# Attention with head mixing: when loaded operands are split, how early they are fetched, and which steps carry a tile's scores

## The chip, the cores and the metric

The kernel runs on one core of a Trainium2 chip. TensorE multiplies matrices into PSUM; VectorE (DVE), ScalarE (ACT) and GpSimd (POOL) work elementwise; SyncE (SP) issues most of the DMAs, in order, from one queue. The metric is the device time of one execution in microseconds (us); lower is better.

## The reference

```
scores = einsum("bhij,hg->bgij", (q @ k^T) / 8, w_pre)     # batch 4, 12 heads, 448 tokens, head size 64
attn   = softmax(scores)                                    # over j
attn   = einsum("bhij,hg->bgij", attn, w_post)
x      = (attn @ v) as [1792, 768]
h      = x @ w_in                                           # then a first feed-forward block, 2048 wide
y      = (h - tanh(h)) @ w_out
out    = y routed to the best of 8 experts by cosine, relu(y @ w1) @ w2, times the expert's probability
```

All is 32-bit floating point. The change lies in the attention alone.

## The kernel before, in words

The program is unrolled Python. A scheduler lays out each engine's instructions: it goes by the order in which they are written, but may place one ahead of others on its engine when it takes its inputs to be ready, and it inserts the waits. On the chip each engine then works strictly through its own list.

Attention handles one batch after the other. A batch has four tiles of query rows (120, 120, 120 and 88), and a tile is worked in *steps* of 10 rows with all 12 heads: 12, 12, 12 and 9 steps, 45 in a batch, 180 in all. Step numbers here count through the program.

- **Scores** (`scores`, L203 to L209). For a pair of heads, six matmuls make q·k from halves kept in 16 bits (qh, ql, kh, kl). The two results go to PSUM banks 0 and 1, are copied into the tile's `S` by ACT (L209), or by DVE (L207) for heads 2, 5, 8 and 11, and only then can the next pair use the banks. Six pairs make a tile; they are spread over the steps of the tile before it.
- **Gather** (`shuffle`, L231). A DMA on the SP queue collects the 120 rows (10 rows by 12 heads) of one step from `S` into `G`. There are four `G` buffers, so the gather of step s + 4 waits until step s has read its own.
- **Premix** (`premix`, L240 to L255). One matmul with `w_pre` into one of three banks, a minimum over j on DVE (L244), the exponential on ACT (L250, followed by a read of its sum), and on odd steps a subtraction on POOL (L255) that makes a second 16-bit half.
- **Normalise and postmix** (L265 to L295). Four steps later, `w_post` scaled by the sums multiplies the transposed exponentials: 4 fp32 matmuls on even steps (the trace counts 8 passes), 12 on 16-bit halves on odd ones. ACT copies the result into `at32` (L294), POOL makes its low half (L295). The banks are 4 and 5 in turn.
- **Values** (`window`, `values`, L305 to L313). When a batch's 45 steps are through, 144 matmuls multiply by v.

Into these steps work is placed that loads and *splits* operands. A fetch issues a DMA on the SP queue into one of three `raw` buffers; a split casts it on ACT and subtracts on POOL or DVE, and so frees the buffer: `fetch_v`/`split_v` (L192, L193), `fetch_pairs`/`split_pairs` for the next batch's q and k (L171 to L177), `fetch_w`/`convert_w` for w_in of the later feed-forward block (three DVE operations L77 to L81, an ACT cast L326, a DVE subtraction L327, and two DMAs out, L350). The table `todo` holds which of them run in which step: `at(s, f, ...)`. A split follows its fetch by 4 steps for v, 2 for q and k, 3 for w_in. Before a step's own work, the loop issues gathers for steps up to s + 3, but those of a new tile only from two steps before its first.

Of the kernel before, what the change touches and what calls it, by code (L numbers as in the profile page):

```python
# [16 lines left out]
AF = mybir.ActivationFunctionType  # L17
ALU = mybir.AluOpType
AX = mybir.AxisListType
# [3 lines left out]
B, H, S, D = 4, 12, 448, 64  # L23
# [11 lines left out]
GB = 4  # L35
# [4 lines left out]
AHEAD = 4  # L40
# [16 lines left out]
def group(t, c):  # L57
    i0, m, _ = TILES[t]
    if m == 120:
        return [i0 + c + 12 * ii for ii in range(10)]  # L60
    if c < 8:
        return [i0 + c + 8 * ii for ii in range(10)]
    return [i0 + 80 + ii for ii in range(8)]
# [26 lines left out]
def halved(u):  # L90

    return u % 2 == 1


def attention(tc, bank, q0, k0, qT, kT, vP, w_pre, w_post, w_in, xd, wind, pos, yg, constants):
    nc = tc.nc
    HW = DM // 2
    with ExitStack() as ctx:
# [121 lines left out]
        def shuffle(b, t, c):  # L220
            i0, m, _ = TILES[t]
            g = gp.tile([120, S], F32, tag="G", name=f"G_{b}_{t}_{c}")
            s = St[b, t]
            n = len(group(t, c))
            if m == 120:
                rows = s[c:c + 12 * 9 + 1:12]
            elif c < 8:
                rows = s[c:c + 8 * 9 + 1:8]
            else:
                rows = s[80:88]  # L230
            nc.sync.dma_start(out=g[:12 * n], in_=rows)  # L231
            G[b, t, c] = g

        mid, sums = {}, {}

        def premix(b, t, c, u):
            r = 12 * len(group(t, c))
            g = G.pop((b, t, c))
            ps = bank((2, 3, 6)[u % 3], 0, 1)
            nc.tensor.matmul(ps[:r, :S], wmix[:r, :r], g[:r], start=True, stop=True)  # L240
            if u % 2 == 0:
                sums[u // 2] = p4.tile([120, 8], F32, tag="st", name=f"st_{u // 2}")
            st, k = sums[u // 2], u % 2
            nc.vector.tensor_reduce(out=st[:r, k:k + 1], in_=ps[:r, :S], axis=AX.X, op=ALU.min)  # L244
            bias = st[:r, k:k + 1]
            if halved(u):
                bias = st[:r, 2 + k:3 + k]
                nc.vector.tensor_scalar(out=bias, in0=st[:r, k:k + 1], scalar1=EXPB, scalar2=None, op0=ALU.add)
            a = A[u % (LAG + 1)]
            nc.scalar.activation(out=a[:r, :S], in_=ps[:r, :S], func=AF.Exp, bias=bias, scale=-1.0,  # L250
                                 accum_out=st[:r, 4 + k:5 + k])
            parts = None
            if halved(u):
                parts = a.bitcast(BF)[:, 1::2], a.bitcast(F16)[:, 0::2]
                nc.gpsimd.tensor_tensor(out=parts[1][:r, :S], in0=a[:r, :S], in1=parts[0][:r, :S], op=ALU.subtract)  # L255
            mid[u] = (a, parts)
# [73 lines left out]
        steps = [(b, t, c) for b in range(B) for t in range(4) for c in range(TILES[t][2])]  # L330
        tiles = [(b, t) for b in range(B) for t in range(4)]
        todo = {}

        def at(s, f, *a):
            todo.setdefault(s, []).append((f, a))

        at(30, load_constants)
        for b in range(B):
            s0 = 45 * b
            for jc in range(4):  # L340
                at(s0 + 1 + 4 * jc, fetch_v, b, jc)
                at(s0 + 5 + 4 * jc, split_v, b, jc)
            if b + 1 < B:
                for u in range(NP // 2):
                    at(s0 + 23 + 4 * u, fetch_pairs, b + 1, u)
                    at(s0 + 25 + 4 * u, split_pairs, b + 1, u)

        def store(pairs):
            for o, i in pairs:
# [20 lines left out]
        in_window, u = {}, 0  # L370
        for b in range(B):
            for k in range(4 if b < B - 1 else 5):
                at(45 * b + 10 + 7 * k, fetch_w, u)
                at(45 * b + 13 + 7 * k, convert_w, u)
                u += 1
            n = 5 if b < B - 1 else 0
            in_window[b] = list(range(u, u + n))
            u += n
        assert u == 2 * FC

        first = {}
        s0 = 0
        for ti, (b, t) in enumerate(tiles):
            first[b, t] = s0
            if ti + 1 < len(tiles):
                ng = TILES[t][2]
                for p in range(NP) if ti else range(AHEAD // 2, NP):
                    at(s0 - 3 + (2 * p + 1) * ng // H if ti else 2 * p - AHEAD, scores, *tiles[ti + 1], p)
            s0 += TILES[t][2]

        def after(s):
            if s % 2 == 0 and 0 <= s - 2 < len(steps):
                normalise([u for u in (s - 2, s - 1) if u < len(steps)])
            if s >= LAG:
                postmix(*steps[s - LAG], s - LAG)
                if steps[s - LAG][1:] == (3, 8) and steps[s - LAG][0] < B - 1:
                    window(steps[s - LAG][0])
# [12 lines left out]
            scores(0, 1, p)  # L410
        nxt = 0
        for s, (b, t, c) in enumerate(steps):
            while nxt < min(s + GB, len(steps)) and first[steps[nxt][:2]] <= s + 2:
                shuffle(*steps[nxt])
                nxt += 1
            premix(b, t, c, s)
            for f, a in todo.pop(s, []):
                f(*a)
            after(s)
        assert not todo  # L420
# [643 lines left out]
def talking_heads_moe(ctx, tc, q0, k0, q, k, v, w_pre, w_post, w_in, w_out, emb, tau, w12, ident_d, tri_d, tokf_d, rowi_d,  # L1064
# [11 lines left out]
    def bank(base, i=None, n=2):  # L1076

        if i is None:
# [11 lines left out]
    ids0 = gc.tile([EARLY[1], EARLY[0]], I32, tag="ids0", name="ids0")  # L1090
    chosen = {}
    attention(tc, bank, q0, k0, q, k, v, w_pre, w_post, w_in, xd, wind, pos, yg,
              ((ident, ident_d), (tokf, tokf_d), (rowi, rowi_d), (iota, iota_d), (thr, thr_d)))
    before = moe1(tc, ctx, bank, xd, wind, w_out, emb, tau, (ident, tri_d, tokf, rowi, iota, thr), yg, pos, keep, ids0,
# [59 lines left out]
```

## Time and profile before

| | |
|---|---|
| median of three runs | 1286.94 us |
| lowest, highest | 1285.57, 1294.75 us |
| the profiled execution | 1288.26 us, of which its span is 1286.0 us |
| stepped part of attention in it | 20.1 to 455.8 us |

The rows read from the profile below are of that one execution. Its time lies 1.3 us over the median. "Waits" rows give an engine's idle time by what ended it; a name such as "PE bank L203" is the engine, the tile that is written and the line of the program.

### The profile page before, as it was taken

Reading aid. Unit: us, or ns where it says so; the run is one execution under the profiler, and the core shown is the slowest. Engines: PE = TensorE matmul, PEld = TensorE weight load, DVE = VectorE, ACT = ScalarE, POOL = GpSimd, SP = SyncE. Lnnn points to the kernel's source line nnn. Section 1 sums busy time; section 2 is a strip of 40 time slices with the busy share of each in tenths; the row PEclk is TensorE's granted clock in tenths of the full one; section 3 lists DMA queues with packets and bytes.
Section 4 is the critical chain, followed back from the end, with each engine's and each line's share of the span. In section 5 each row is a group of like instructions: output and inputs, shape, how many; then the busy total and the mean of one; then the engine's idle time right before and its main releaser. Section 6 shows DMA issues by size and latency. Waiting matters only on the chain.

```text
span 1286.0 us, 23742 instructions
## 1 busy us (share of the span) xinstructions
PE 1193.8 (93%) x8624; PEld 837.4 (65%) x8648; DVE 855.1 (66%) x1895; ACT 729.0 (57%) x1499; POOL 707.3 (55%) x594
## 2 busy tenths in 40 slices
PE   8999899989999988999899999999978899999995
PEld 3655565555555664566566666667876678989883
DVE  5877687768767829977766456745878345566662
ACT  6777687667767744444455444545556334555551
POOL 5887678577767753433443335334566355566550
PEclk8999999999999999999999999999998999999998
DMA  6555746555574476223001000100043656678640
GB/s 212 174 182 146 221 162 190 175 182 184 148 208 162 116 236 219 93 97 131 25 1 50 1 25 1 50 1 1 2 140 133 212 194 205 213 242 263 229 159 22
DMA packets 82854, 173.90 MB, mean 135 GB/s; under 512 B 12155, under 2 KB 60155, under 8 KB 82728
## 3 DMA queue, kind: packets, MB, share of 16 engines
q1 hardware_dynamic: 76986, 160.75, 38.7%
q0 software_dynamic: 5472, 11.43, 3.0%
q8 instruction: 70, 1.15, 0.4%
q14 instruction: 56, 0.46, 0.1%
q10 hardware_dynamic: 270, 0.12, 0.0%
HBM read 110.79 MB, written 23.30 MB: 104 GB/s over the span
## 4 chain that ended last, share of the span: by engine, by line
PE 59%; DVE 16%; DMA 12%; ACT 6%; issue 3%; POOL 2%; SPq 0%; POOLq 0%; ACTq 0%; DVEq 0%
PE bank L561 11%; PE bank L533 10%; PE bank L913 7%; PE bank L240 7%; PE bank L937 7%; PE bank L290 7%; DMA G<-S 3%; PE bank L203 3%; DMA raw_v<-in_v_dram 3%; PE bank L305 2%; DVE g L547 2%; DMA wor<-in_w_out_dram 2%; DVE g L548 2%; DVE wl_a L903 2%; ACT A L250 1%
## 5 line engine op out<-in xcount | busy, mean ns | idle before, releaser
L561 PE MATMUL bank<-ghl,whl 128*128 128x512 f32 (+1 forms) x1152 | 258.1, 376 | 9.3 <-POOL ghl L551 4.9
L561 PEld LDWEIGHTS bank<-ghl,whl 128*128 128x128 f32 x1152 | 199.6, 192 | 50.8 <-POOL ghl L551 6.3
L483 POOL TENSOR_TENSOR whl<-wo,whl 128x768 fp32r<-128x768 f32 x64 | 118.8, 1857 | 177.2 <-ACT whl L482 177.1
L295 POOL TENSOR_TENSOR at<-at 128x480 f16<-128x480 f32 x180 | 177.0, 996 | 51.9 <-ACT at L294 50.2
L240 PE MATMUL bank<-G,wmix 120*120 120x448 f32 x360 | 176.7, 575 | 11.3 <-DMA G<-S 11.3
L290 PE MATMUL bank<-wr,A 120*128 120x120 f32 (+4 forms) x1800 | 175.3, 246 | 5.2 <-ACT x L312 3.0
L250 ACT ACTIVATE A<-bank,st 120x448 f32<-120x448 f32 x180 | 114.3, 636 | 53.5 <-DVE st L244 22.2
L244 DVE TENSOR_REDUCE st<-bank 120x1 f32<-120x448 f32 x180 | 111.2, 618 | 46.3 <-PE bank L240 45.1
L903 POOL TENSOR_TENSOR wl_a<-wr_a,wh_a 128x768 bf16<-128x768 f32 x56 | 93.1, 1670 | 70.4 <-ACT wh_a L902 70.0
L551 POOL TENSOR_TENSOR ghl<-g,ghl 128x512 fp32r<-128x512 f32 (+1 forms) x64 | 76.6, 1197 | 99.7 <-ACT ghl L550 99.7
L903 DVE TENSOR_TENSOR wl_a<-wr_a,wh_a 128x768 bf16<-128x768 f32 x56 | 83.1, 1484 | 61.9 <-ACT wh_a L902 61.9
L533 PEld LDWEIGHTS <-wih 128*128 128x128 f16 x768 | 72.4, 99 | 76.3 <-issue 15.9
L290 PEld LDWEIGHTS bank<-wr,A 120*128 120x128 f32 (+1 forms) x720 | 94.5, 198 | 34.5 <-issue 17.8
L294 ACT COPY at<-bank 128x480 f32<-128x480 f32 x180 | 101.3, 567 | 25.0 <-PE bank L290 24.7
L902 ACT CAST wh_a<-wr_a 128x768 f16<-128x768 f32 x112 | 92.6, 829 | 39.2 <-PE bank L937 35.2
L543 DVE SCALAR_TENSOR_TENSOR g<-bank,u 128x512 f32<-128x512 f32 (+1 forms) x64 | 39.9, 623 | 108.6 <-ACT d L540 105.2
L255 POOL TENSOR_TENSOR A<-A 120x448 f16<-120x448 f32 (+1 forms) x90 | 84.4, 938 | 32.0 <-ACT A L250 13.4
L482 ACT CAST whl<-wo 128x768 fp32r<-128x768 f32 x64 | 53.1, 831 | 71.1 <-PE bank L561 53.0
L533 PE MATMUL bank<-mxh,wih 128*128 128x512 f16 (+1 forms) x384 | 85.1, 358 | 5.4 <-DVE d L544 4.2
L290 PEld LDWEIGHTS <-A 120*128 120x128 bf16 (+2 forms) x1080 | 63.1, 100 | 40.9 <-issue 33.9
L550 ACT CAST ghl<-g 128x512 fp32r<-128x512 f32 (+1 forms) x64 | 36.2, 566 | 91.6 <-DVE g L548 81.0
L913 PE MATMUL bank<-xph_a,wh_a 128*128 128x208 f16 (+5 forms) x336 | 87.2, 262 | 0.0
(214 smaller groups left out, 2701.3 us busy)
## 6 DMA issues: line engine op xcount, KB each, us to landing
wr_a<-in_w_dram SPq DMA_DIRECT2D x64, 768.0 KB
G<-S SPq DMA_DIRECT2D x176, 210.0 KB
raw_w<-in_w_in_dram SPq DMA_DIRECT2D x32, 384.0 KB
wor<-in_w_out_dram SPq DMA_DIRECT2D x16, 768.0 KB
raw_v<-in_v_dram SPq DMA_DIRECT2D x16, 384.0 KB
yg<-row SPq DMA_DIRECT2D x3, 1540.0 KB
raw_q<-in_q_dram SPq DMA_DIRECT2D x9, 448.0 KB
raw_k<-in_k_dram SPq DMA_DIRECT2D x9, 448.0 KB
```

The lines of the kernel that those rows point to most:

```text
L240: nc.tensor.matmul(ps[:r, :S], wmix[:r, :r], g[:r], start=True, stop=True)
L244: nc.vector.tensor_reduce(out=st[:r, k:k + 1], in_=ps[:r, :S], axis=AX.X, op=ALU.min)
L250: nc.scalar.activation(out=a[:r, :S], in_=ps[:r, :S], func=AF.Exp, bias=bias, scale=-1.0, accum_out=st[:r, 4 + k:5 + k])
L290: nc.tensor.matmul(ps[:, jc * r:jc * r + r], x[:r, js], w[:r].rearrange("p (a b) -> p a b", b=10)[:, :, :n], start=(i == 0), stop=(i == le ...
L294: nc.scalar.copy(at32[:, :, t0:t0 + n], v)
L295: nc.gpsimd.tensor_tensor(out=atl[:, :, t0:t0 + n], in0=at32[:, :, t0:t0 + n], in1=ath[:, :, t0:t0 + n], op=ALU.subtract)
L483: nc.gpsimd.tensor_tensor(out=w[:, 1], in0=wo[f], in1=w[:, 0].bitcast(F32), op=ALU.subtract)
L533: nc.tensor.matmul(h, u[f][:, c], X[b][v][:, c, :N], start=(i == 0), stop=(i == len(seq) - 1))
L561: nc.tensor.matmul(Y[b][c][:, :N], w[:, u, 128 * c:128 * c + 128], hl[:, v, :N], start=(f == 0 and i == 0), stop=(f == FC - 1 and i == 2))
L902: nc.scalar.copy(wh, raw)
L903: (nc.vector if j else nc.gpsimd).tensor_tensor(out=wl, in0=raw, in1=wh, op=ALU.subtract)
L913: nc.tensor.matmul(h, w[u][:, 128 * c:128 * c + 128], XP[e][v][:, c, :N], start=(i == 0), stop=(i == len(seq) - 1))
```

## The change

Four things. The splits are wrapped in `behind`, which ties every instruction that a split puts on DVE or ACT behind the step's own minimum (DVE) and exponential (ACT); in a step's list they now run ahead of the other entries. The splits and fetches move: v is fetched in steps 5, 9, 13, 17 of a batch (it was 1, 5, 9, 13) and split 4 steps later as before; q and k are fetched in the same steps 23, 27, 31 but split 4 steps later, not 2; w_in is fetched 5 steps ahead, not 3, and split one step earlier. The score pairs of the next tile stand in steps -2, -1, 1, 2, 4, 6 from the tile's first (it was -2, 0, 2, 4, 6, 8); in the 9-step tile in -2, -1, 0, 1, 2, 4 (it was -3, -1, 0, 2, 3, 5). And the gathers of a new tile may be issued three steps before its first, not two.

```diff
-        mid, sums = {}, {}
+        mid, sums, latest = {}, {}, {}
...
-            nc.vector.tensor_reduce(out=st[:r, k:k + 1], in_=ps[:r, :S], axis=AX.X, op=ALU.min)
+            latest["dve"] = nc.vector.tensor_reduce(out=st[:r, k:k + 1], in_=ps[:r, :S], axis=AX.X, op=ALU.min)
...
-            nc.scalar.activation(out=a[:r, :S], in_=ps[:r, :S], func=AF.Exp, bias=bias, scale=-1.0,
-                                 accum_out=st[:r, 4 + k:5 + k])
+            latest["act"] = nc.scalar.activation(out=a[:r, :S], in_=ps[:r, :S], func=AF.Exp, bias=bias, scale=-1.0,
+                                                 accum_out=st[:r, 4 + k:5 + k])
...
+        def behind(f, *a):
+
+            with ExitStack() as order:
+                for x in latest.values():
+                    order.enter_context(tc.issue_after(x.ins))
+                f(*a)
+
...
             for jc in range(4):
-                at(s0 + 1 + 4 * jc, fetch_v, b, jc)
-                at(s0 + 5 + 4 * jc, split_v, b, jc)
+                at(s0 + 9 + 4 * jc, behind, split_v, b, jc)
+                at(s0 + 5 + 4 * jc, fetch_v, b, jc)
             if b + 1 < B:
                 for u in range(NP // 2):
+                    at(s0 + 27 + 4 * u, behind, split_pairs, b + 1, u)
                     at(s0 + 23 + 4 * u, fetch_pairs, b + 1, u)
-                    at(s0 + 25 + 4 * u, split_pairs, b + 1, u)
...
-                at(45 * b + 10 + 7 * k, fetch_w, u)
-                at(45 * b + 13 + 7 * k, convert_w, u)
+                at(45 * b + 7 + 7 * k, fetch_w, u)
+                at(45 * b + 12 + 7 * k, behind, convert_w, u)
...
-                    at(s0 - 3 + (2 * p + 1) * ng // H if ti else 2 * p - AHEAD, scores, *tiles[ti + 1], p)
+                    at(s0 - 2 + 8 * p * ng // 60 if ti else 2 * p - AHEAD, scores, *tiles[ti + 1], p)
...
-            while nxt < min(s + GB, len(steps)) and first[steps[nxt][:2]] <= s + 2:
+            while nxt < min(s + GB, len(steps)) and first[steps[nxt][:2]] <= s + 3:
...
-            for f, a in todo.pop(s, []):
+            for f, a in sorted(todo.pop(s, []), key=lambda x: x[0] is not behind):
                 f(*a)
```

Three places show what the scheduler makes of it. On ACT in batch 0 before the change, the cast of the second k load of batch 1 (`raw_k_1_1`) stands behind the exponential of step 27 (`A2`; the one of step 28 is `A3`):

```order
L294 COPY at32_97<-bank4_113_1014 128x48x10
L294 COPY at32_97<-bank5_115_1042 128x48x10
L250 ACTIVATE A2_107,st_13_994<-bank2_114_1023,st_13_994 120x448
L175 CAST kh_120<-raw_k_1_1_1031 128x896
L326 ACTIVATE wh_2_1036<-bank7_1_98 128x384
L250 ACTIVATE A3_108,st_14_1061<-bank3_116_1059,st_14_1061 120x448
L209 COPY S_0_3_876<-bank0_117_1064 88x448
```

After the change both casts of that pair of loads stand behind the exponential of step 31 (`A1`), the q one first:

```order
L250 ACTIVATE A1_106,st_15_1127<-bank3_128_1161,st_15_1127 120x448
L175 CAST qh_118<-raw_q_1_1_1048 128x896
L175 CAST kh_120<-raw_k_1_1_1050 128x896
L250 ACTIVATE A2_107,st_16_1196<-bank6_130_1194,st_16_1196 120x448
L294 COPY at32_97<-bank4_131_1206 128x48x10
L294 COPY at32_97<-bank5_133_1230 128x48x10
```

The casts moved four steps down, and no work of the step stands between them and its exponential.

On the SP queue in batch 3 before the change, `G_3_0_9` to `G_3_0_11` are the gathers of steps 144 to 146, and `G_3_1_0` is that of step 147, the first of a new tile:

```order
L231 DMA G_3_0_9_5151<-S_3_0_4387 120x1x448
L133 DMA raw_w_27_5271<-in_w_in_dram 128x384
L231 DMA G_3_0_10_5184<-S_3_0_4387 120x1x448
L133 DMA raw_v_3_3_5362<-in_v_dram 128x768
L133 DMA raw_w_28_5483<-in_w_in_dram 128x384
L231 DMA G_3_0_11_5205<-S_3_0_4387 120x1x448
L133 DMA raw_w_29_5679<-in_w_in_dram 128x384
L231 DMA G_3_1_0_5261<-S_3_1_4679 120x1x448
L231 DMA G_3_1_1_5263<-S_3_1_4679 120x1x448
```

The same stretch after it, from `G_3_0_9`:

```order
L231 DMA G_3_0_9_5155<-S_3_0_4414 120x1x448
L231 DMA G_3_0_10_5188<-S_3_0_4414 120x1x448
L231 DMA G_3_0_11_5211<-S_3_0_4414 120x1x448
L231 DMA G_3_1_0_5234<-S_3_1_4679 120x1x448
L231 DMA G_3_1_1_5261<-S_3_1_4679 120x1x448
L231 DMA G_3_1_2_5295<-S_3_1_4679 120x1x448
L133 DMA raw_v_3_2_5367<-in_v_dram 128x768
L231 DMA G_3_1_3_5326<-S_3_1_4679 120x1x448
```

Four loads of v and w_in that stood between and ahead of these gathers are gone from there; the next load now stands behind the gather of step 149.

On ACT at the end of batch 0 before the change, in steps 32 to 36, `S_1_0` is the score buffer of batch 1's first tile and `bank4`, `bank5` are postmix results; the list begins with the two score copies of that tile's first pair and the exponential of step 33 (`A3`):

```order
L209 COPY S_1_0_1225<-bank0_133_1226 120x448
L209 COPY S_1_0_1225<-bank1_134_1227 120x448
L250 ACTIVATE A3_108,st_16_1186<-bank2_132_1213,st_16_1186 120x448
L294 COPY at32_97<-bank5_135_1236 128x48x10
L326 ACTIVATE wh_3_1263<-bank7_1_98 128x384
L294 COPY at32_97<-bank4_137_1276 128x48x10
L250 ACTIVATE A4_109,st_17_1257<-bank3_136_1255,st_17_1257 120x448
L250 ACTIVATE A0_105,st_17_1257<-bank6_138_1285,st_17_1257 120x448
L209 COPY S_1_0_1225<-bank1_140_1292 120x448
L294 COPY at32_97<-bank5_141_1301 128x48x10
L250 ACTIVATE A1_106,st_18_1320<-bank2_142_1318,st_18_1320 120x448
L209 COPY S_1_0_1225<-bank0_143_1323 120x448
```

After it, the first copy of that tile's first pair stands just ahead of this list, which begins with the exponentials of steps 33 (`A3`) and 34 (`A4`) and the pair's second copy:

```order
L250 ACTIVATE A3_108,st_16_1196<-bank2_132_1215,st_16_1196 120x448
L250 ACTIVATE A4_109,st_17_1249<-bank3_134_1247,st_17_1249 120x448
L209 COPY S_1_0_1252<-bank1_136_1254 120x448
L326 ACTIVATE wh_3_1224<-bank7_1_98 128x384
L294 COPY at32_97<-bank4_137_1270 128x48x10
L209 COPY S_1_0_1252<-bank1_140_1292 120x448
L294 COPY at32_97<-bank5_141_1301 128x48x10
L250 ACTIVATE A0_105,st_17_1249<-bank6_138_1279,st_17_1249 120x448
L175 CAST qh_118<-raw_q_1_2_1173 128x896
L175 CAST kh_120<-raw_k_1_2_1175 128x896
L250 ACTIVATE A1_106,st_18_1320<-bank2_142_1318,st_18_1320 120x448
L209 COPY S_1_0_1252<-bank0_143_1323 120x448
```

The second copy of the first pair now stands behind the exponentials of steps 33 and 34, and the copy of the third pair (the last row) stands behind two casts of loads and the exponentials of steps 35 (`A0`) and 36 (`A1`).

## Rows read from the trace of the kernel before

**Rows 1.** The page: busy us, share of the span and instructions of each engine.

```profile
...
PE 1193.8 (93%) x8624; PEld 837.4 (65%) x8648; DVE 855.1 (66%) x1895; ACT 729.0 (57%) x1499; POOL 707.3 (55%) x594
...
```

**Rows 2.** Stretches: length, busy PE, PEld, DVE, ACT, POOL, granted clock, DMA share, GB/s.

```profile
...
20.10:455.80 435.70, 407.10 (x3055) 248.60 (x3055) 327.24 (x918) 313.49 (x749) 315.42 (x313) 0.97 0.57 173
...
```

**Rows 3.** Waits of TensorE, 22 to 444 us: total us, times, longest.

```profile
...
PE bank L203 <- ACT S L209: 9.7, 7, 2.2
PE bank L240 <- DMA G<-S: 6.5, 7, 1.9
PE bank L290 <- ACT x L312: 3.0, 2, 2.0
PE bank L203 <- DVE S L207: 3.0, 3, 1.4
PE bank L290 <- ACT at L294: 1.5, 1, 1.5
PE bank L290 <- DVE wr L272: 0.6, 1, 0.6
```

**Rows 4.** Waits of ScalarE, 20 to 456 us, same columns.

```profile
...
ACT vh L192 <- DMA raw_v<-in_v_dram: 13.3, 10, 2.7
...
ACT kh L175 <- DMA raw_k<-in_k_dram: 7.7, 3, 2.8
...
```

**Rows 5.** Timeline, 73.5 to 84.5 us: start, length, instruction, idle time before it.

```profile
...
74.12 0.34 SPq L171 DMA_DIRECT2D raw_k<-in_k_dram  x1
...
75.73 0.64 ACT L250 ACTIVATE A<-bank,st 120x448 f32<-120x448 f32 x1 [0.53 <-DVE st L248]
...
76.27 0.19 ACT L250 ACTIVATION_READ_ACCUMULATOR A<-bank,st 120x1 f32 x1
...
79.09 0.94 ACT L175 CAST kh<-raw_k 128x896 f16<-128x896 f32 x1 [2.63 <-DMA raw_k<-in_k_dram]
...
81.50 0.78 PE L203 MATMUL bank<-kh,qh 64*88 64x448 f16 x2 [2.13 <-ACT S L209]
...
```

**Rows 6.** Stretches, same columns: first and last of five at half clock.

```profile
...
84.20:87.60 3.40, 3.40 (x17) 2.19 (x17) 2.70 (x9) 2.65 (x7) 3.40 (x4) 0.50 0.83 255
...
374.30:377.70 3.40, 3.40 (x19) 2.57 (x18) 0.69 (x2) 2.17 (x5) 3.40 (x4) 0.50 0.69 185
...
```

**Rows 7.** Waits of the SP queue, 380 to 392 us.

```profile
...
SPq L133 <- POOL vl L193: 5.6, 2, 3.1
...
```

**Rows 8.** Timeline of the SP queue, 374 to 396 us.

```profile
...
387.65 0.33 SPq L133 DMA_DIRECT2D raw_w<-in_w_in_dram  x1
388.08 5.64 SPq L231 DMA_DIRECT2D G<-S  x5
...
```

**Rows 9.** Timeline, 91 to 104 us: two score products in neighbouring steps.

```profile
...
97.37 0.61 DVE L207 COPY S<-bank 120x448 f32<-120x448 f32 x1
...
98.04 0.55 PE L203 MATMUL bank<-kh,qh 64*120 64x448 f16 x2 [1.11 <-DVE S L207]
...
```

**Rows 10.** Chain of waits, 211 to 231 us: start, length, what.

```profile
...
218.28 0.80 PE bank L240 x2
...
223.40 0.71 PE bank L203 x6
224.11 1.08 PE bank L290 x8
...
225.94 0.63 PE bank L290 x12
...
```

**Rows 11.** ScalarE by line, 22 to 444 us: busy us, mean ns, idle before.

```profile
...
L294 ACT COPY at<-bank 128x480 f32<-128x480 f32 x169 | 95.3, 568 | 18.2 <-PE bank L290 18.1
L209 ACT COPY S<-bank 120x448 f32<-120x448 f32 (+1 forms) x116 | 58.6, 530 | 4.0 <-PE bank L203 3.7
...
L326 ACT ACTIVATE wh<-bank 128x384 f16<-128x384 f32 x31 | 15.2, 489 | 20.3 <-DVE bank L81 20.3
...
L175 ACT CAST kh<-raw_k 128x896 f16<-128x896 f32 x9 | 8.5, 942 | 8.4 <-DMA raw_k<-in_k_dram 7.7 <-PE bank L203 0.6
```


## The prediction

> **What bounds the kernel now.** I read the page first: TensorE is busy for 1193.8 us of a 1286.0 us span [rows 1], so an edit pays only where it shortens a wait of TensorE. The change touches the 180 attention steps alone, and there TensorE is busy 407.1 of 435.7 us [rows 2]: 28.6 us idle is all the wait that the stage holds. The view of TensorE's waits says who ends them; 25 us up to 444 us, in six kinds [rows 3]. The reader should then ask of each kind what its releaser had been doing, since "ACT S" names only the copy that came last. ScalarE's own waits answer it: it stood 13.3 us, in ten waits, for loads of v and 7.7 us, in three, for loads of k [rows 4]. One instance in order of time: the k load is issued at 74.12, ScalarE finishes an exponential at 76.46 and then stands 2.63 us in front of the k cast, and TensorE, which needs a score copy queued behind that cast, stands 2.13 us at 81.50 [rows 5]. Last the granted clock: five stretches of 3.4 us in this stage after the first steps run at 0.50, that is 1.2 instead of 2.4 GHz, though TensorE is busy all through the two shown [rows 6]; each begins within 5 us behind one or two of these waits. At half speed 3.4 us do the work of 1.7, so each costs about 1.7 us, 8.5 in all.
>
> **The change part by part.**
>
> *Splits tied and later, loads earlier.* The same casts, subtractions and DMAs run, none is added. The second k cast moves from behind the exponential of step 27 to that of step 31, its load from before the gather of step 31 to behind that of step 32: about three steps more to land, some 5 us (two steps with one score product among them take 0.80 + 0.71 + 1.08 and 0.80 + 0.63, 4.0 us [rows 10]), where 2.6 us were missing [rows 5]. The v loads after the first gain as much, and they come into steps in which the window before no longer holds the raw buffers. What goes: the score waits for ACT copies (9.7), the postmix waits for ACT and DVE (1.5 and 0.6) [rows 3]. One of the seven score waits, 0.6 us, has another cause (below) and stays out: **-11.2**. What hides the loads is the steps in between; if the cover failed, the 11.2 would come back.
>
> *The window.* TensorE waits 3.0 us in two places for the x copies behind the values product [rows 3]; in those places v casts stand among the x copies now, and later they don't. A cast is some 0.9 us long [rows 11], and the rest was a wait for a load: **-2.5**, with 0 and -3.0 as bounds.
>
> *Gathers.* TensorE waits 6.5 us for G [rows 3]. In the worst of these the SP queue held a w_in fetch back for a raw buffer that a v subtraction on POOL had yet to free, 5.6 us in two waits [rows 7]; the fetch went at 387.65, and five gathers had to go behind it from 388.08 on [rows 8]. The new order has none of these fetches there. Moreover the last scores come two steps earlier and the gather may go one earlier: **-6.5**, bounds 0 and -6.5.
>
> *What is late next, on the SP queue.* A split and the next fetch of q and k now fall into the same step, so the k fetch and a w_in fetch wait in the SP queue for the split that has just been started, and the gathers of steps 33, 78 and 123 wait behind them. The nearest row is the same event above: 1.9 us was the longest G wait [rows 3]. Bounds 0 and 1.9 for each of three places; I take 0.8, since here the buffers come free about two steps before the gather is needed: **+2.4**.
>
> *What is late next, in the score banks.* Score pairs in neighbouring steps find the same two banks, so the second needs the copies of the first within one step. Before, 9 such neighbours occur, all around the 9-step tiles, and three of them stall: the three waits for DVE copies (3.0 [rows 3]), of which one is shown (the copy ends at 97.98, TensorE goes at 98.04 [rows 9]), and the 0.6 left out above; 3.6 us, 0.40 each. After, 32 occur, so 12.8 us by that mean; by the longest, 1.4 [rows 3], 45, and by those that don't stall, 0. I also follow one place, steps 34 to 37, with time 0 at the premix of 34. TensorE takes 0.80 for a premix, 0.71 for a score pair, 1.08 or 0.63 for a postmix [rows 10]; ACT 0.73 for an exponential with its read [rows 5], 0.53 for a score copy, 0.57 for a postmix copy, 0.49 for the w_in cast, 0.94 for a q or k cast [rows 11]. The pair's product ends at 1.5; ACT copies one bank until 2.05, does the exponentials of 33 and 34 and ends the second copy at 4.05. TensorE would be ready at 3.4: it waits 0.65. From there ACT does the w_in cast, copies, the exponential of 35, both casts and the exponential of 36, and ends the copy of the third pair at 10.1, TensorE being ready at 8.8: 1.3 more. Followed in the same way, the other places where a cast stands ahead of a copy (steps 11, 23, 44 of batches 0 and 2; 11, 14 and 37 of batch 1; 11 and 14 of batch 3) give 0.4 to 2.0 each; all together 13. Two ways agree on 13; less the 3.6 of now: **+9.4**. ACT is busy only 313.49 of 435.70 us [rows 2], so this is order, not load.
>
> *The clock.* With the long waits gone the half-clock stretches should go, -8.5; two places keep some 2 us of wait in 5 us, and I leave two stretches: **-5.1**, bounds 0 and -8.5.
>
> Sum: -11.2 - 2.5 - 6.5 + 2.4 + 9.4 - 5.1 = **-13.5 us**. The profiled execution took 1288.26, so it would take 1274.8; on the median of 1286.94 that is **1273.4**.
>
> **The rivals.**
>
> *The covers hold, and neighbours cost little.* Six of nine neighbours don't stall now, and those that do wait for DVE, on which the splits are tied behind the minimum afterwards. With 4 us for neighbours and gathers together and no half clock: -20.2 - 3.6 + 4 - 8.5 = -28, **1259**. Against it: the walk above, where ACT, not DVE, is late.
>
> *The waits only change their names.* ACT holds the same casts in the same stage, and tied behind the exponential they stand ahead of score copies oftener. If the neighbours cost 0.67 each, and the clock falls as often as now, the gain is gone (20.2 + 3.6 = 23.8 against 21.4 + 2.4): **1287**. That also covers a change that doesn't do what it says, where a fetch written earlier is held back by its raw buffer in the SP queue and lands no earlier.
>
> *Slower: the two banks become the bound.* If every neighbour stalls as the one shown, 1.11 us [rows 9], 32 cost 35 us: -20.2 - 3.6 + 35 + 2.4 = +14 with the clock as now, **1301**. It is slower from 0.67 per neighbour on with the clock as now, from 0.93 with the clock mended. For it: the walk found such waits in half of the places. Against it: six of nine cost nothing.
>
> *The clock as a price of short waits.* So far no half-clock stretch stands behind the neighbours' waits of about 1.1 and 1.4 us, but only behind longer ones or two together. If it fell once for each of the 15 tiles whose scores are now gathered, 15 times 1.7 is 25.5 for the present 8.5: -20.2 + 2.4 + 9.4 + 17 = +9, **1296**. The Trainium skill, "TensorE: Matmul & The Clock Gate", section "A second HAM failure mode: psum-queue depth-cycling", says that a kernel which cycles through PSUM banks and idles briefly but often between groups of matmuls can have its clock swing between the two levels. By that rule this is the outcome; the trace has the brief idling, ten bank waits of the scores [rows 3], but not the swing.
>
> **How the numbers follow.** The forecast, 1264 to 1281 around 1273.4: 0.50. Covers hold, 1259: 0.15. Only names change, 1281 to 1290: 0.24. Banks become the bound: 0.08. Clock: 0.03. A measurement of this kernel can tell about 1% from no change, 12.9 us, so 1274.1 is the edge: of the forecast's 0.50 some 0.29 lies beneath it. Faster by over 1%: 0.15 + 0.29 = 0.44, and 0.05 of the case of names falls there through a gain in gathers alone, 0.49. Slower by over 1%: 0.03 of clock and 0.06 of banks, 0.09. The rest, 0.42, is the same. The range leaves out 0.08 below and 0.11 above: **1259 to 1286**.
>
> **What would show it.** Right: ACT's waits for raw_v and raw_k under 4 us in the stage (21 now); TensorE's waits for G before 444 us under 4; the score waits for ACT and DVE copies at 10 to 15 us and now in neighbouring steps, above all at steps 35 and 37 of a batch, with exponentials and casts ahead of the copy; one to three half-clock stretches. Wrong: score waits beyond 24 us (the banks), G waits that stay at 6 us with SP waits for kl or ql subtractions (the queue), or ACT still in front of casts whose load has not landed.

## The result, and the profile after

The changed kernel takes 1273.59 us (median of four runs, 1270.14 to 1276.38), the kernel before 1288.12 in the same comparison: a ratio of 0.9878, 95% interval 0.9833 to 0.9923. The forecast was 1273.4. The profiled execution took 1276.38 us, its span is 1274.6. Behind line 336 the line numbers are 7 higher than before (L357 was L350).

The page's busy time, columns as in [rows 1]:

```profile
PE 1195.8 (94%) x8648; PEld 841.4 (66%) x8648; DVE 860.2 (67%) x1895; ACT 728.8 (57%) x1499; POOL 706.7 (55%) x594
```

The stretch of the 180 steps, columns as in [rows 2], and the one half-clock stretch that is left behind the first steps:

```profile
21.20:437.70 416.50, 406.41 (x3055) 251.30 (x3055) 328.65 (x916) 314.82 (x749) 316.93 (x314) 0.98 0.59 181
206.50:216.74 10.24, 10.24 (x46) 5.77 (x45) 4.42 (x16) 5.13 (x12) 4.87 (x6) 0.50 0.50 145
```

The steps take 416.5 us where they took 435.7 [rows 2], 19.2 less. TensorE's idle time in them falls from 28.6 us to 10.1. Its busy time is the same within 0.7 us, but only since two shifts cancel in it: less of it runs at half clock, and the score products take longer (both below). TensorE's waits from 22 to 434 us say which idle time went:

```profile
PE bank L240 <- DMA G<-S: 4.8, 9, 0.8
PE bank L290 <- DVE wr L272: 1.7, 4, 0.5
PE bank L203 <- ACT S L209: 1.2, 1, 1.2
PE bank L290 <- ACT x L312: 0.8, 2, 0.4
```

Against [rows 3]: the score products wait 1.2 us once, where they waited 12.7 in ten places; the postmix waits 1.7 us for DVE in place of 2.1 for ScalarE and DVE; the x copies cost 0.8 for 3.0; only the gathers keep most of theirs, 4.8 of 6.5. The window of [rows 3] ends at 444 us, though, and in the last steps behind it the kernel before waits for gathers again (first row, 444 to 456 us); the second row is the changed kernel's whole stage behind the first step, 22.2 to 445.7 us:

```profile
PE bank L240 <- DMA G<-S: 3.6, 4, 2.3
```

```profile
PE bank L240 <- DMA G<-S: 5.9, 10, 1.1
```

So over the stage the gathers' waits fall from 10.1 to 5.9 us. ScalarE's waits for loads, 20 to 446 us, are down from the 21.0 us of [rows 4] to one:

```profile
ACT kh L175 <- DMA raw_k<-in_k_dram: 1.2, 1, 1.2
```

Of the whole span that is 19.2 less in the steps, 1.1 more ahead of them (the first premix starts at 21.2, not 20.1), and 6.7 more behind them, in code that the change does not touch: 836.9 us from the last premix to the end, 830.2 before. That part differs between executions of one order of instructions by more than this (last section).

### The profile page after: what moved, and what is told of

The parts are those of the page before. It is cut to its first block, busy times and chain, and to the rows that moved or that the text cites. A ratio compares the mean times of both kernels' runs of the same rounds, so it can differ in the third digit from the quotient of the medians.

```text
span 1274.6 us, 23764 instructions
## 1 busy us (share of the span) xinstructions
PE 1195.8 (94%) x8648; PEld 841.4 (66%) x8648; DVE 860.2 (67%) x1895; ACT 728.8 (57%) x1499; POOL 706.7 (55%) x594
## 4 chain that ended last, share of the span: by engine, by line
PE 66%; DVE 15%; DMA 9%; ACT 4%; issue 3%; POOL 2%; SPq 0%; POOLq 0%; ACTq 0%; DVEq 0%
PE bank L568 11%; PE bank L540 10%; PE bank L290 9%; PE bank L240 8%; PE bank L920 8%; PE bank L944 7%; PE bank L203 5%; PE bank L305 4%; DMA G<-S 3%; DMA wor<-in_w_out_dram 3%; DVE g L554 2%; DVE wl_a L910 2%; DVE g L555 2%; DVE wo L81 1%; DVE wo L79 1%
## 5 line engine op out<-in xcount | busy, mean ns | idle before, releaser
L240 PE MATMUL bank<-G,wmix 120*120 120x448 f32 x360 | 171.5, 562 | 8.3 <-DMA G<-S 8.3
L290 PE MATMUL bank<-wr,A 120*128 120x120 f32 (+4 forms) x1800 | 171.8, 243 | 3.7 <-DVE wr L272 2.7
L910 POOL TENSOR_TENSOR wl_a<-wr_a,wh_a 128x768 bf16<-128x768 f32 x56 | 92.3, 1657 | 73.7 <-ACT wh_a L909 73.5
L290 PEld LDWEIGHTS bank<-wr,A 120*128 120x128 f32 (+1 forms) x720 | 91.5, 193 | 35.8 <-issue 19.8
L920 PE MATMUL bank<-xpl_a,wh_a 128*128 128x208 bf16 (+5 forms) x336 | 87.8, 264 | 0.0
```

The costliest lines, as they stand in the source:

```text
L290: nc.tensor.matmul(ps[:, jc * r:jc * r + r], x[:r, js], w[:r].rearrange("p (a b) -> p a b", b=10)[:, :, :n], start=(i == 0), stop=(i == le ...
L910: (nc.vector if j else nc.gpsimd).tensor_tensor(out=wl, in0=raw, in1=wh, op=ALU.subtract)
L920: nc.tensor.matmul(h, w[u][:, 128 * c:128 * c + 128], XP[e][v][:, c, :N], start=(i == 0), stop=(i == len(seq) - 1))
```

## The experiments

"The steps" is the time from the first premix to the last in the one profile that each kernel has. Ratios are to the kernel before, on the same chip. "Half clock" is how long the granted clock stood at 0.50 in the steps. An undisturbed score pair's six products start within 0.80 us there and within 0.43 elsewhere, so the last column takes off half of that time; it is an estimate of the steps at full clock.

| kernel | time, us | ratio (95%) | steps, us | half clock, us | less its half |
|---|---|---|---|---|---|
| kernel before | 1288.12 | | 435.6 | 23.1 | 424.1 |
| changed kernel | 1273.59 | 0.9878 (0.9833 to 0.9923) | 416.5 | 13.7 | 409.7 |
| old score steps | 1272.05 | 0.9921 (0.9885 to 0.9958) | 420.7 | 18.9 | 411.3 |
| score steps only | 1274.30 | 0.9934 (0.9901 to 0.9967) | 420.9 | 13.5 | 414.2 |
| untied | 1282.13 | 1.0003 (0.9972 to 1.0033) | 429.7 | 16.2 | 421.5 |
| gathers two ahead | 1273.07 | 0.9929 (0.9893 to 0.9965) | 417.6 | 13.7 | 410.8 |
| ties only | 1279.46 | 0.9959 (0.9934 to 0.9983) | 420.1 | 16.6 | 411.8 |
| third split later | 1268.27 | 0.9871 (0.9813 to 0.9930) | 413.3 | 6.2 | 410.2 |
| fetch one later | 1273.34 | 0.9900 (0.9839 to 0.9961) | 415.6 | 6.8 | 412.2 |
| whole pairs | 1270.77 (one run) | | 417.8 | 5.7 | 414.9 |
| gather first | 1266.36 | 0.9858 (0.9812 to 0.9905) | 412.0 | 6.8 | 408.6 |
| v ties only | 1271.96 | 0.9906 (0.9876 to 0.9936) | 423.6 | 17.1 | 415.0 |
| ties and scores | 1270.54 | 0.9900 (0.9873 to 0.9927) | 416.0 | 5.7 | 413.2 |
| six steps | 1279.93 | 0.9944 (0.9919 to 0.9968) | 426.7 | 6.8 | 423.3 |

Most of these intervals overlap, so it is the waits in the profiles, not the times, that tell the parts of the change from each other.

**Undo the scores.** In the changed kernel:

```diff
-at(s0 - 2 + 8 * p * ng // 60 if ti else 2 * p - AHEAD, scores, *tiles[ti + 1], p)
+at(s0 - 3 + (2 * p + 1) * ng // H if ti else 2 * p - AHEAD, scores, *tiles[ti + 1], p)
```

> The changed kernel with the score pairs at their old steps; ties, loads and gathers as changed. The 180 steps take 416.5 us from the first premix to the last in the changed kernel's profile, 435.7 in the kernel before. Theory A, the prediction's: neighbouring pairs cost 9.4 us net, so without them the steps take 405 to 410 us. Theory B: neighbours cost little, since a pair's half can go as soon as its own bank is free; the changed kernel holds 1.2 us of waiting for a score copy and some 4.8 us of pairs whose halves run one behind the other (1.2 to 1.4 instead of 0.71 us). Then these go, the waits for G grow from 4.8 to 6 or 8, and the steps take 413 to 419 us.

Measured 420.7 us, outside both ranges. Theory A falls, since the steps got longer (2.6 of the 4.2 us is the clock). Theory B was too small in the gathers: TensorE's waits, 22 to 434 us, in this kernel:

```profile
PE bank L240 <- DMA G<-S: 10.6, 9, 2.2
PE bank L290 <- DVE wr L272: 1.8, 5, 0.4
```

With the last scores two steps later, G costs 10.6 us, not 4.8. Ties and loads alone, without the scores, save 14.9 us of steps.

**The scores alone.** The same two lines the other way round, in the kernel before:

> The kernel before with the new score steps alone; ties, loads and the gathers' distance as before. Theory A: 32 neighbours cost what the prediction says and meet the late loads too: 435.7 + 9.4 = 445 us for the 180 steps, ACT still 21 us in front of casts of v and k. Theory B: neighbours cost 2 to 5 us and the earlier gathers give some back: 433 to 438 us. Either way ScalarE's waits for raw_v and raw_k stay at 18 to 24 us.

Both theories fall: 420.9 us, 14.7 less than before (4.8 of it the clock), from the part that the prediction had at +9.4. TensorE's waits, 22 to 434 us, and then ScalarE's for loads:

```profile
PE bank L290 <- ACT at L294: 6.6, 7, 2.5
PE bank L240 <- DMA G<-S: 3.6, 5, 1.2
...
PE bank L203 <- ACT S L209: 0.7, 1, 0.7
PE bank L203 <- DVE S L207: 0.5, 1, 0.5
```

```profile
ACT vh L192 <- DMA raw_v<-in_v_dram: 10.7, 8, 2.9
ACT kh L175 <- DMA raw_k<-in_k_dram: 3.9, 2, 2.9
```

ScalarE still stands 14.6 us in front of unlanded loads (21.0 before, less than the 18 to 24 expected), but the score copies are seldom queued behind those casts any more. What now stands behind them is the copy of a postmix, which TensorE misses later. One instance of this kernel in order of time:

```profile
150.96 0.83 ACT L192 CAST vh<-raw_v 128x768 f16<-128x768 f32 x1 [2.95 <-DMA raw_v<-in_v_dram]
...
152.91 0.79 PE L290 MATMUL bank<-wr,A 120*128 120x120 f16 x12 [1.48 <-ACT at L294]
```

A wait of 2.95 us on ScalarE comes through as 1.48; before, 2.63 came through as 2.13 [rows 5].

**No ties.** In the changed kernel, splits at their new steps and first in them:

```diff
-                for x in latest.values():
-                    order.enter_context(tc.issue_after(x.ins))
                 f(*a)
```

> The changed kernel without the ties: the splits stand in the same steps and first in their step, but nothing holds them behind the exponential and the minimum. Theory B1, the distance of the loads is what pays: the loads have still landed, ScalarE waits under 2 us for raw_v and raw_k, and the steps take 414 to 419 us (416.5 with ties). Theory B2, the ties pay: casts and subtractions go ahead of exponential and minimum, TensorE waits again for score copies and wr, 5 us or more in all, and the steps take 421 to 428 us.

B1 falls, B2 holds and by a little more: 429.7 us, and in time no gain at all. The written step does not set a cast's place; the scheduler moves an untied cast ahead. The cast of the fourth v load, written into step 21, stands here in step 7 (first row), in the changed kernel in step 22 (second fence):

```profile
36.47 0.83 ACT L192 CAST vh<-raw_v 128x768 f16<-128x768 f32 x1 [3.66 <-DMA raw_v<-in_v_dram]
```

```profile
64.19 0.86 ACT L192 CAST vh<-raw_v 128x768 f16<-128x768 f32 x1
```

**Gathers two steps ahead**, `<= s + 2` for `<= s + 3`, and **the fetches of q and k one step later**, `23 + 4 * u + (u > 0)` for `23 + 4 * u`:

> The changed kernel with the gathers allowed two steps ahead as before, not three. Theory B: the earlier last scores alone carry the gathers; G waits stay at 4 to 6 us (4.8 in the changed kernel) and the steps take 416 to 418 us. Theory C: the third step is what removes them; G waits return to the 6.5 us of the kernel before or more, and the steps take 418 to 421 us.

> The changed kernel with the second and third fetch of q and k one step behind the split whose buffers they take, not in its step. The G waits at the 34th step of three batches (0.84, 0.52, 0.78 us) are put down to the SP queue held by these fetches. Theory H, that is so: the three go, 2 us in all, and the loads land no later, as they were held until the buffers came free; the steps take 413 to 416 us. Theory I, the fetch then stands behind more gathers: k lands later, ScalarE waits 2 us or more in front of k casts, and the steps take 417 to 422 us.

Both leave the order of instructions on all five engines as it is in the changed kernel, so they test nothing of their theories. What they give is two further executions of the changed kernel: steps of 417.6 and 415.6 us, at full clock 410.8 and 412.2 for the 409.7 above, so a difference of 2 or 3 us says little. And the third step of the gathers does nothing.

**The ties alone**, in the kernel before:

> The kernel before with the ties alone: splits first in their step and behind its exponential and minimum, everything at the old steps. 180 steps: 435.6 us before, 416.5 with all changes, 429.7 with all but the ties. Theory D, the ties put the casts later on ScalarE than the steps say, and that is the distance which pays: ScalarE's waits for raw_v and raw_k fall from 20 us to under 8, and the steps take 420 to 428 us. Theory E, the ties pay only with the loads moved ahead: the casts still stand before unlanded loads, 12 us or more of such waits, and the steps take 430 to 437 us.

D holds: 420.1 us, and ScalarE's waits for loads from 20 to 446 us are one row:

```profile
ACT kh L175 <- DMA raw_k<-in_k_dram: 0.5, 2, 0.3
```

The tie itself puts the casts far enough behind, at the old steps and with the old loads. At full clock these steps, 411.8 us, lie within the spread of the changed kernel's three executions. In time the ties alone gave 5.3 us, the scores alone 9.1; score copies still wait 4.2 us in two places.

**Ties and scores, old loads:**

> The kernel before with ties and with the new score steps; splits and loads keep their old steps. Ties alone gave 420.1 us, the score steps alone 420.9, all changes 416.5 (415.6 and 417.6 in two further executions of the same order). Theory N, the loads further ahead add nothing once the ties hold the casts back: the steps take 414 to 419 us, ScalarE's waits for raw_v and raw_k are under 3 us. Theory O, they are needed: a cast or two stand before unlanded loads, 4 us or more of such waits, and the steps take 419 to 424 us.

N holds: 416.0 us and no wait for raw_v or raw_k at all. The earlier loads and later steps add nothing that these runs can tell: at full clock it is 413.2 us for 409.7 to 412.2.

**Ties on v alone** (the splits of q, k and w_in without `behind`, still first in their steps):

> The changed kernel with the ties on the v splits alone; q, k and w_in splits keep their new steps, untied. Without any tie ScalarE stood 19.8 us in front of v casts and 2.1 us in front of k casts, and the steps took 429.7 us. Theory L, it is v that the ties hold: the v casts' waits go, the steps take 416 to 420 us. Theory M, untied q and k splits alone put casts ahead of score copies and exponentials: ScalarE waits 2 to 8 us for q and k, TensorE for at and score copies, and the steps take 421 to 427 us.

M by the profile (423.6 us; ScalarE waits 13.2 us for q and k, more than expected; score products wait 8.9). The times do not separate it from the changed kernel (1271.96), so what the q, k and w_in ties are worth in time stays open.

**Whole pairs.** In the changed kernel each product of a score pair is tied behind the one written ahead of it:

```diff
+            last = []
...
+                    with ExitStack() as order:
+                        if last:
+                            order.enter_context(tc.issue_after(last[-1].ins))
+                        last.append(nc.tensor.matmul(ps[:m, :S], u[o:o + 64, p, i0:i0 + m], v[o:o + 64, p], start=(i == 0), stop=(i == 2)))
```

> The changed kernel with the six products of each score pair held in their written order, the two banks in turn, so that a pair can start only when both banks are free, as the prediction's walk had it. In the changed kernel some pairs were ordered three and three, and go 0.15 to 0.70 us apart, 4.8 us in all. Theory J, this order is what saved the change from the 13 us of the walk: TensorE now waits 8 to 14 us for score copies, and the steps take 420 to 428 us. Theory K, the walk had the copies too late anyway: TensorE waits 2 to 6 us for score copies in place of the 4.8 us, and the steps take 414 to 418 us.

By its range K holds, 417.8 us in the one execution there is: score copies are waited for 2.3 us in five places. But the edit does not do what the expectation says. It keeps the six products in their written order; it does not hold the first until both banks are free. Where a pair's second bank is late, part of a postmix now runs between its first and second product, as the timeline of this kernel has it:

```profile
93.22 0.40 PE L207 MATMUL bank<-kh,qh 64*120 64x448 f16 x1
93.55 0.44 PE L294 MATMUL bank<-wr,A 120*128 120x120 f16 x5
93.92 0.40 PE L207 MATMUL bank<-kh,qh 64*120 64x448 f16 x1
```

**Six steps in a row.**

```diff
-at(s0 - 2 + 8 * p * ng // 60 if ti else 2 * p - AHEAD, scores, *tiles[ti + 1], p)
+at(s0 - 2 + p if ti else 2 * p - AHEAD, scores, *tiles[ti + 1], p)
```

> The changed kernel with a tile's six score pairs in six steps in a row: 70 neighbouring pairs by the formula, where the changed kernel has 34 and the kernel before 9. In the changed kernel the neighbours cost 6.0 us: 4.8 of pairs whose halves go apart and 1.2 of waiting, 0.18 each. Theory P, the price of a neighbour stays as it is: 13 us in all, and the steps take 420 to 427 us (416.5 in the changed kernel). Theory Q, the prediction's banks: once several pairs stand in a row, each needs the copies of the one ahead of it, and a neighbour costs 0.4 to 1.1 us: 28 us or more in all, and the steps take 435 us or more. Theory R, TensorE does other work meanwhile and gathers come earlier still: under 8 us for neighbours, and the steps take 414 to 419 us.

P by its range, at its upper edge: 426.7 us. (By the formula the changed kernel has 34 neighbours; the prediction counted 32.) The 36 further ones cost 10.2 us, 0.28 each, and 13.6 or 0.38 at full clock, just under Q's 0.4. But Q's mechanism is excluded: the waits for score copies are only 1.3 of it (2.5 for 1.2). The rest is score products that take longer (79.7 us busy for 77.1), and longer waits for gathers and for DVE.

**Third split later**, and **the gather ahead of the k fetch:**

```diff
-at(s0 + 27 + 4 * u, behind, split_pairs, b + 1, u)
+at(s0 + 27 + 4 * u + (b == 1 and u == 2), behind, split_pairs, b + 1, u)
```

> The changed kernel with one split moved: the third of q and k in the second batch goes from step 35 to step 36, so that its k load has landed. In the changed kernel ScalarE waits 1.2 us for it and TensorE 1.2 us for a score copy, and a half-clock stretch of 10.24 us begins there. Theory F, that wait sets the clock off: both go, the steps take 409 to 412 us (416.5 less 1.2 and 5.1). Theory G, the stretch would come anyway, behind some other short wait: the wait goes, a stretch of 3.4 to 10.2 us stays between 180 and 235 us, and the steps take 413 to 416 us.

The second kernel has this edit, and `23 + 4 * u + 3 * (u > 0)` as the step of the fetches of q and k:

> The kernel with the third split of the second batch at step 36, and the second and third fetch of q and k three steps later than in the changed kernel, so that the gather of the 34th step of a batch stands ahead of the k fetch in the SP queue (one step later had left the order of the queue as it was). Theory H again: the G waits at the 34th step (0.84, 0.52, 0.78 us in the changed kernel; 1.09 and 0.92 with the split moved) come from that queue and go. If k still lands in time, the steps take 410 to 413 us (413.3 with the split alone moved); if not, ScalarE waits 1 us or more in front of k casts, TensorE for score copies, and they take 414 to 418 us. If the G waits stay, Theory H is wrong.

The first: the wait for raw_k goes, a wait of 0.96 us for a score copy comes a step earlier, and there is no half-clock stretch; 413.3 us lies in G's range, though without G's stretch. That does not show F, since the changed kernel's order without any edit also ran once without the stretch (last section). The second: H holds this time. The SP queue around the 34th step in the changed kernel, and in this one:

```profile
80.31 0.34 SPq L171 DMA_DIRECT2D raw_k<-in_k_dram  x1
81.69 0.34 SPq L133 DMA_DIRECT2D raw_w<-in_w_in_dram  x1
82.11 6.69 SPq L231 DMA_DIRECT2D G<-S  x5
```

```profile
81.47 0.34 SPq L171 DMA_DIRECT2D raw_q<-in_q_dram  x1
81.91 0.81 SPq L231 DMA_DIRECT2D G<-S  x1
82.84 0.41 SPq L171 DMA_DIRECT2D raw_k<-in_k_dram  x1
83.36 5.52 SPq L231 DMA_DIRECT2D G<-S  x4
```

The three G waits at the 34th step go, and three of 0.59, 0.18 and 0.44 us come a step later: 1.2 us for the 2.1. Its ratio, 0.9858, is the lowest here, but the times do not tell it from the changed kernel's 0.9878.

## Why the prediction was right, and where its sum was not

The total is met, but by a sum whose largest positive term is wrong, and that it is met so closely is luck. The steps lost 19.2 us, not 13.5; in the profiled execution 6.7 of that came back behind the steps, in code that the change does not touch, and 1.1 ahead of them. The measured terms below are from the profile of the changed kernel, in us, against the groups of rows named.

| term of the sum | predicted | measured |
|---|---|---|
| splits tied and loads earlier | -11.2 | -8.9: 11.8 [rows 3] to 2.9 |
| the window | -2.5 | -2.2 |
| gathers, and the SP queue | -6.5 + 2.4 | -4.2: 6.5 to 4.8 up to 444 us, 3.6 to 1.1 behind it |
| score banks | +9.4 | +0.8: DVE waits 3.0 to 0; score products 3.8 longer at full clock |
| clock, five stretches | -5.1 | -3.4: five of 3.4 us to one of 10.24 |
| clock, first steps | none | -1.3: 6.0 us at half clock to 3.4 |
| sum | -13.5 | -19.2 |

Of the four signs of being right that it names, two came (ScalarE's waits for loads, 1.2 us; one stretch) and two did not (waits for G under 4 us; score waits of 10 to 15).

**The step that failed: "Two ways agree on 13; less the 3.6 of now: +9.4".** Most places were right (a pair went apart at step 23 of batches 1 and 3, not of 0 and 2), the size not. Pairs do run late at steps 11, 35, 37 and 44 of batches 0 and 2, 11 and 14 of batches 1 and 3, but by 0.15 to 0.70 us each, 4.8 in all outside the half-clock stretch. The walk of steps 34 to 37 beside the changed kernel's timeline (the premix of step 34 starts at 88.48):

```profile
89.37 0.40 PE L203 MATMUL bank<-kh,qh 64*120 64x448 f16 x2
...
91.84 0.54 ACT L209 COPY S<-bank 120x448 f32<-120x448 f32 x1
91.92 0.40 PE L203 MATMUL bank<-kh,qh 64*120 64x448 f16 x1
...
92.44 0.35 PE L203 MATMUL bank<-kh,qh 64*120 64x448 f16 x1
...
97.17 0.40 PE L203 MATMUL bank<-kh,qh 64*120 64x448 f16 x1
97.30 0.54 ACT L209 COPY S<-bank 120x448 f32<-120x448 f32 x1
...
97.89 0.35 PE L203 MATMUL bank<-kh,qh 64*120 64x448 f16 x1
```

The walk had TensorE ready at 3.4 and the copy done at 4.05; the trace has 3.44 and 3.90. For the third pair it had 8.8 and 10.1; the trace has 8.69 and 9.36. So the first was right, and the second 0.7 us too late. But the walk let the whole pair wait for both banks. The scheduler had ordered this pair three and three, as the order of TensorE's instructions shows (weight loads left out; bank_139 and bank_140 are the two banks):

```
L240 MATMUL bank_138_1279<-G_2_11_1192,wmix 120x448
L203 MATMUL bank_139_1291<-kh,qh 120x448
L203 MATMUL bank_139_1291<-kh,ql 120x448
L203 MATMUL bank_139_1291<-kl,qh 120x448
L203 MATMUL bank_140_1292<-kh,qh 120x448
L203 MATMUL bank_140_1292<-kh,ql 120x448
L203 MATMUL bank_140_1292<-kl,qh 120x448
```

So the bank that is free is filled while the other is copied, and what is lost is that the halves no longer run side by side: the six starts spread over 0.89 us at step 35 and 1.09 at step 37, 0.43 in an undisturbed pair. That does not appear among the waits at all, it is busy time of the score products, x524 in both (first the changed kernel, then the one before):

```profile
21.20:437.70 416.50, 77.10 (x524) 0.98 0.59 181
```

```profile
20.10:455.80 435.70, 71.60 (x524) 0.97 0.57 173
```

At half clock lie 5.4 of the 77.1 us and 2.0 of the 71.6; without half of each they are 74.4 and 70.6, so the products take 3.8 us longer. With the 3.0 us of DVE waits that went, the term is +0.8.

The Trainium skill, "TensorE: Matmul & The Clock Gate", section "The mechanism", says that products on different row groups of the array run together and that matmuls start and end in program order. The rows agree with both: an undisturbed pair's two halves start together, a pair ordered three and three goes one half behind the other.

The prediction's other mean, 0.40 for each neighbour that stalled before, was not a price of neighbours. Six of [rows 3]'s seven score waits for ScalarE stood behind a cast that had waited for its load, and in two of the three for VectorE (330.91 us and the one shown, 98.04) it had just run some 3 us of split work, the k subtraction and the w_in conversion. Bunching the scores removes nearly all of them by itself (1.2 us left). In "whole pairs", where a pair keeps its written order, score copies are waited for 2.3 us and not 8 to 14, as other work goes between. What a pair would cost that waits for both banks, as in the walk, no run here shows.

**Ties and loads: the right size for the wrong reason.** "What hides the loads is the steps in between" was not what decided. Without ties the steps in between did not exist (the scheduler took the casts back, 429.7 us); with ties at the old steps, and old loads, ScalarE's waits for loads were down to 0.5 us; and the scores alone took most of them off TensorE. Two parts, 14.9 and 14.7 us of steps when done singly, give 19.2 together (at full clock 12.8 and 9.9, and 14.4 together): they remove the same wait, one by moving the cast, one by moving the copy behind it.

**Gathers.** The three places on the SP queue came as predicted, 2.1 us (0.84, 0.52, 0.78) for 2.4, and "gather first" shows that the queue is their cause. But the -6.5 was not earned where it was predicted: up to 434 us six other G waits of 0.3 to 0.8 us stayed or came, and "the gather may go one earlier" had no effect on the order. The net -4.1 is met by the waits of the last steps, which the prediction's window left out.

**The clock.** One stretch, within the one to three foreseen, but three times as long.

**The rivals.** The likeliest mechanism was in the end that of "the covers hold, and neighbours cost little"; its 1259 was not reached since 4.8 us of G waits, 4.8 of late halves and the half-clock stretch stayed. "Only the names change" and "the two banks become the bound" are excluded by the waits and by "six steps". The clock as a price of short waits did not come: 16 short waits in the stage, one stretch. The kernel before had 21, longer ones among them, and five stretches; that is more of a swing than the prediction's "but not the swing" allows.

Steps and times do not agree to the microsecond: the profiled execution of the kernel before took 1288.26 us, while its medians beside the experiments were 1283 to 1288, so 19.2 is at the upper end of what the change saves. The times give 10 to 15. The kernel before was profiled only once.

## What to carry to other kernels

Before pricing a tighter reuse of two PSUM banks, look at how the products are ordered: a pair that may go apart, or that lets other work between, pays in tenths of a microsecond of busy time, not in the whole wait for a copy. A step number in the program moves an engine's queue only where something holds the instruction there; an untied cast went fifteen steps back and gave the whole gain away. And where two edits attack one wait from both ends, do not add their prices: each alone gave some three quarters of what both gave in the steps.

## What the runs showed of the hardware

**Clock.** The same order of instructions ran three times. In two profiles a half-clock stretch of 10.24 us began behind a score wait of 1.2 and 1.5 us at step 37 of the second batch; in the third ("fetch one later") the wait was 1.49 us and the clock there stayed at full:

```profile
206.50:216.70 10.20, 8.71 (x68) 5.83 (x68) 7.60 (x25) 7.16 (x17) 8.22 (x9) 1.00 0.67 207
```

So a wait of that size does not decide by itself, and a term for it in a sum is a chance, not a price.

**VectorE behind GpSimd.** From the last premix to the end the three executions took 836.9, 826.3 and 837.7 us. Some 3 us of the difference are the clock: 40.7, 34.6 and 41.6 us of these stretches were at half clock. Another part lies in the experts' 56 subtractions on VectorE, with a median of 1.20 us; in the changed kernel four took 4.4 to 6.0. One of them, beside GpSimd and the wait of TensorE that followed:

```profile
1161.18 6.00 DVE L910 TENSOR_TENSOR wl_a<-wr_a,wh_a 128x768 bf16<-128x768 f32 x1
1161.52 4.84 POOL L910 TENSOR_TENSOR wl_a<-wr_a,wh_a 128x768 bf16<-128x768 f32 x3
...
1167.53 0.54 PE L973 MATMUL bank<-ident,ot_a 128*104 128x128 f32 x3 [3.43 <-DVE rl_a L925]
```

VectorE's one subtraction ends only behind three of GpSimd in a row. The 13 that ran beside no GpSimd instruction took 0.96 us at most. In the execution with the short tail two of these took over 2.5 us, not four. The Trainium skill, "SBUF — State Buffer", section "SBUF: two separate sides", says that a VectorE instruction with two SBUF inputs and a GpSimd instruction that reads SBUF exclude each other for a whole instruction. This row agrees in kind, but here VectorE's instruction ended behind three, not one.
